# q and k loaded as pairs of tokens, one transpose per half, fillers in banks of their own, and a new order

## The chip, the cores and the metric

The kernel runs on one core of one Trainium2 chip. The metric is the device time of one execution in microseconds, the median of three runs. The engines are named as in the profile: PE is TensorE, DVE is VectorE, ACT is ScalarE, POOL is GpSimd, SP is SyncE (it issues most of the DMAs; ScalarE can issue some).

## The reference, cut to what matters

Attention over four batches of eight heads, 768 tokens and 64 columns a head. Each token sees its neighbours within 15 tokens, and 24 block keys (the maximum of k over 32 tokens) with the block means of v. The result, as 3072 rows of 512, goes through a feed-forward layer with 2048 columns.

```python
k_sum = k.reshape(B, H, nb, block, D).max(axis=3)
v_sum = v.reshape(B, H, nb, block, D).mean(axis=3)
scores_l = scale * np.matmul(q, k.transpose(0, 1, 3, 2))
mask_l = np.abs(pos[:, None] - pos[None, :]) < window
scores_s = scale * np.einsum('bhsd,bhnd->bhsn', q, k_sum) + np.log(block)
scores_all = np.concatenate([np.where(mask_l, scores_l, -1e9), scores_s], axis=-1)
# softmax over scores_all, times [v, v_sum]
...
h = x @ w_in
g = h - np.tanh(h)
return (g @ w_out).astype(np.float32)
```

## The kernel before, in words

The unit of work is a half of a batch, `u` of 8 (384 tokens, three tiles of 128), and a group `g` of four heads (two groups). For each (batch, group), `load_qk` fetches q and k in four pieces each of 192 KB on 128 partitions, and `turn` turns every piece with two transposes of VectorE into `qT` and `kT`, which hold columns on partitions. In the transposed tiles the tokens of a piece lie 24 apart. `top` takes the block maxima of k on VectorE and puts copies of them among the keys. `scores` is 48 multiplications into four PSUM banks, `softmax` works on pairs of heads `p` (four blocks for a half: two in each group): a minimum with the mask on VectorE, exponentials on ScalarE, the inverse of the sums, a scaling on any of three engines. `transpose_probs` turns the probabilities on TensorE (a `p turn`, seen as `ident,prob`), `values` multiplies them with v (`probT,vw`). The probabilities live in a ring of three buffers. The block means of v come from `sum_chunks` on TensorE, with the columns of a small constant tile (`wh`).

The feed-forward layer runs behind it in units (u, f), f being one of 16 column blocks: `moe_in` (`pH<-o,wf` in the first half), the activation, and `moe_out` into three banks `pY`. The weights are converted and split into high and low parts on VectorE, ScalarE and GpSimd as the first halves run (`convert`).

The program is a list of tasks with engines and costs (`Plan`). For the program that runs here the order of the tasks is written out, `ORDER`, and so is the engine of each task that may run on several, `ON`. `follow` goes through the tasks in this order and keeps a clock of its own for each engine. Where a TensorE task would start later than TensorE is free, it puts in fillers before it, multiplications of the unit matrix `ident` with itself (`keep_warm`), as many as its own costs say fit in the gap. Before, a filler counts as 0.214 us with a gap of 0.1, fillers stand anywhere in the first 100 us (`WARM`), and they write the bank `pS1`, which the scores use as well (`warm_bank`).

A second program behind a branch repeats the work in another way when a check at the end of the first asks for it; it did not run here.

Of the kernel before, what the change touches and what calls it, by code (L numbers as in the profile page):

```python
# [23 lines left out]
WARM = 100.0  # L24

# [64 lines left out]
class Plan:  # L90

    SEEN = {PE: 0.2, ACT: 0.19, DVE: 0.16, POOL: 0.1, SP: 0.85}
    QUEUE = 3.0
    LEAVES = {"scores": 0.105, "values": 0.105, "top turn": 0.17, "key turn": 0.105, "mean turn": 0.19, "sum": 0.105, "seen turn": 0.08}  # L100

    def __init__(self):
        self.tasks, self.rings, self.place, self.banks, self.count = [], {}, {}, set(), {}
        self.writer, self.readers, self.touch, self.first = {}, {}, {}, {}

    def ring(self, tag, bufs, base):
        self.place[base] = (self.rings.setdefault(tag, []), bufs)

    def add(self, kind, costs, go, r=(), w=()):
        t = Task()  # L110
        t.index, t.kind, t.costs, t.go = len(self.tasks), kind, costs, go
        n = self.count[kind] = self.count.get(kind, -1) + 1
        t.name = kind, n
        t.after, t.order = set(), set()
        t.banks = {key[0] for key in (*r, *w)} & self.banks
        self.tasks.append(t)
        for key in r:
# [7 lines left out]
        for base in dict.fromkeys(key[0] for key in (*r, *w)):  # L125
# [15 lines left out]
            self.touch.setdefault(base, []).append(t)  # L141
        t.after.discard(t)
        t.order.discard(t)
        t.order -= t.after
        return t

    def follow(self, idle):

        tasks = [self.tasks[n] for n in ORDER]
        free = dict.fromkeys((PE, DVE, ACT, POOL, SP), 0.65)  # L150
        dma, held, left = 0.0, {DVE: 0.0, POOL: 0.0}, 0.0
        clock, used, seen, done = Clock(), {}, {}, []
        begin = None
        for t in tasks:
            e = next(iter(t.costs)) if len(t.costs) == 1 else {"D": DVE, "A": ACT, "P": POOL, "S": SP}[ON[t.index]]
            assert all(a in seen for a in (*t.after, *t.order)), t.name
            t.engine, t.cost = e, t.costs[e]
            now = max([free[e]] + [seen[a] for a in t.after] + [at for b in t.banks for a, at in used.get(b, {}).items() if a != e])
            if e == PE:
                cost, go = idle  # L160
                if now > free[PE]:
                    begin = begin or tasks[0].out + self.SEEN[POOL]
                    free[PE] = max(free[PE], min(now, begin))
                while free[PE] < WARM and now - free[PE] > 2 * cost + 0.1:
                    d = Task()
                    d.after, d.order, d.go, d.engine, d.start = (), (), go, PE, free[PE]
                    d.out = clock.run(free[PE], cost)
                    free[PE] = d.out + 0.1
                    done.append(d)
                now = max(now, free[PE])  # L170
                t.cost += left if t.kind in ("in", "out") else 0.0
                left = self.LEAVES.get(t.kind, 0.0)
            elif SP in t.costs:
                now = max(now, dma - self.QUEUE)
            elif e == POOL:
                now = max(now, held[DVE])
                held[POOL] = now + t.cost
            elif e == DVE and t.kind in HELD:
                now = max(now, held[POOL])
                held[DVE] = now + t.cost  # L180
            t.start = now
            if SP in t.costs:
                t.out = free[e] = now + t.issue
                t.moves = max(dma, now + t.ahead)
                dma = t.moves + t.cost
                seen[t] = dma + self.SEEN[SP]
            else:
                t.out = free[e] = clock.run(now, t.cost) if e == PE else now + t.cost
                seen[t] = t.out + self.SEEN[e]
            for b in t.banks:  # L190
                used.setdefault(b, {})[e] = t.out + self.SEEN[e]
            done.append(t)
        return done

    def schedule(self, idle):
# [50 lines left out]
        while total:  # L246
# [20 lines left out]
            if e == PE and idle is not None:  # L267
                cost, go = idle
                if now > free[PE]:
                    free[PE] = max(free[PE], min(now, getattr(tasks[0], "out", now) + self.SEEN[POOL]))  # L270
                while free[PE] < WARM and now - free[PE] > 2 * cost + 0.1:
                    d = Task()
                    d.after, d.order, d.behind = tasks[:1], (), ()
                    d.start, d.engine, d.go = free[PE], PE, go
                    d.out = clock.run(free[PE], cost)
                    free[PE] = d.out + 0.1
                    done.append(d)
                now = max(now, free[PE])
# [61 lines left out]
def program(  # L340
# [14 lines left out]
    P = 128  # L355
# [393 lines left out]
    def raw_buf(which, b, g, j):  # L749
# [9 lines left out]
        if base not in made_by:  # L759
            buf(base, tag, [P, 4, JQ, D])  # L760
# [567 lines left out]
```

## Time and profile before

| | us |
|---|---|
| median of three runs | 665.31 |
| the three runs | 663.7, 665.31, 667.69 |
| the profiled execution | 663.14 |
| its span, first to last instruction | 661.4 |
| TensorE busy | 637.0 |
| VectorE busy | 469.8 |
| ScalarE busy | 452.8 |
| mean granted TensorE clock | 0.989 of full |

The span is a single core's. Busy times are sums over the whole span; the views by stretch tell where they lie. All work is recorded by one helper, line 57 of the kernel, so rows are told apart by their tiles. [...]

### The profile page before, as it was taken

How to read it: one execution, taken by the hardware profiler on the slowest of the kernel's cores; microseconds unless marked ns; L12 is line 12 of the kernel's file. 1: busy time of each engine (PE TensorE's matmuls, PEld its weight loads, DVE VectorE, ACT ScalarE, POOL GpSimd, SP SyncE). 2: the span in 40 equal slices, each digit the busy share in tenths (PEclk: the TensorE clock that was granted, in tenths of full speed). 3: DMA queues.
4: the chain of work that ended last, by engine and by line, in shares of the span. 5: the costliest groups of instructions: out<-in, count | busy, mean ns of one | idle time of the engine just before them, and what ended most of it. 6: DMA issues, size and time to landing. Idle time of an engine off the chain costs nothing.

```text
span 661.4 us, 15152 instructions
## 1 busy us (share of the span) xinstructions
PE 637.0 (96%) x5323; PEld 534.8 (81%) x5323; DVE 469.8 (71%) x1395; ACT 452.8 (68%) x1357; POOL 165.5 (25%) x240
## 2 busy tenths in 40 slices
PE   6789899999999999999999999999999999999997
PEld 6665556678889789999887889999888899999885
DVE  7879999999999894648768884457678844232363
ACT  1568888978898765554789865555798853444874
POOL 1111310214301412215354422211443203202311
PEclk9789999999999999999999999999999999999999
DMA  8648777865577776667534255557424045355101
GB/s 279 192 138 234 204 223 228 249 195 170 166 256 263 242 247 205 208 214 214 157 120 140 68 177 179 171 171 238 136 79 124 33 160 183 135 188 164 43 7 51
DMA packets 103329, 113.25 MB, mean 171 GB/s; under 512 B 43984, under 2 KB 71120, under 8 KB 103248
## 3 DMA queue, kind: packets, MB, share of 16 engines
q1 hardware_dynamic: 102240, 110.53, 53.3%
q10 hardware_dynamic: 1008, 1.70, 0.7%
q8 instruction: 43, 0.70, 0.4%
q14 instruction: 38, 0.31, 0.2%
HBM read 88.87 MB, written 20.97 MB: 166 GB/s over the span
## 4 chain that ended last, share of the span: by engine, by line
PE 76%; DVE 12%; DMA 7%; issue 2%; ACT 2%; POOL 1%; SPq 1%; DVEq 0%; POOLq 0%; ACTq 0%
PE pY L57 34%; PE pH L57 33%; PE pS L57 6%; DVE tmp L57 3%; PE pX L57 3%; DVE wf L57 2%; DMA wraw<-in_moe_w_out_dram 2%; DMA wraw<-scr 2%; DVE qT L57 1%; DVE prob L57 1%; DVE wraw L57 1%; DMA tmp<-in_v_dram 1%; DMA wh<-in_v_dram 1%; DVE kT L57 1%; DMA wraw<-in_moe_w_in_dram 1%
## 5 line engine op out<-in xcount | busy, mean ns | idle before, releaser
L57 ACT ACTIVATE prob<-prob,stat 128x120 f32<-128x120 f32 x296 | 109.6, 385 | 43.3 <-DVE stat L57 40.4
L57 PE MATMUL pH<-wf,wraw 128*128 128x384 f32 x552 | 116.2, 338 | 0.6 <-DMA wraw<-scr 0.4
L57 PE MATMUL pY<-wl,gh 128*128 128x512 f32 x288 | 113.4, 394 | 0.1
L57 PEld LDWEIGHTS pH<-wf,wraw 128*128 128x128 f32 x552 | 97.6, 188 | 6.8 <-ACT gu L57 0.6
L57 PE MATMUL pY<-wh,gh 128*128 128x512 f32 x204 | 84.5, 414 | 0.2 <-DVE gh L57 0.2
L57 PE MATMUL pY<-wh,gl 128*128 128x512 f32 x204 | 80.9, 396 | 0.0
L57 PE MATMUL pY<-wg,gh 128*128 128x512 f32 x168 | 68.8, 409 | 0.0
L57 PE MATMUL pY<-wg,gl 128*128 128x512 f32 x168 | 66.7, 397 | 0.2 <-DVE gl L57 0.2
L57 ACT ACTIVATE gu<-gu 128x384 f32<-128x384 f32 x128 | 65.5, 519 | 2.0
L57 PE MATMUL pH<-o,wf 128*128 128x384 f32 x188 | 65.9, 446 | 0.2 <-DVE wf L57 0.2
L57 PEld LDWEIGHTS pY<-wl,gh 128*128 128x128 f32 x288 | 54.2, 188 | 9.9 <-DVE wl L57 0.6
L57 POOL TENSOR_TENSOR gl<-gu,gh 128x384 fp32r<-128x384 f32 x29 | 30.3, 1046 | 119.3 <-ACT gh L57 79.6
L57 PE MATMUL pH<-wg,wraw 128*128 128x384 f32 x288 | 56.1, 338 | 0.1
L57 PEld LDWEIGHTS pH<-wg,wraw 128*128 128x128 f32 x288 | 50.7, 188 | 3.2 <-DMA wraw<-scr 0.6
L57 POOL TENSOR_TENSOR gu<-gu,gt 128x384 f32<-128x384 f32 x32 | 33.4, 1046 | 75.6 <-ACT gu L57 57.9
L57 ACT ACTIVATE gv<-pH 128x384 f32<-128x384 f32 x43 | 20.9, 487 | 37.5 <-PE pH L57 35.9
L57 PEld LDWEIGHTS pH<-o,wf 128*128 128x128 f32 x188 | 34.6, 191 | 14.5 <-issue 1.0
L57 PEld LDWEIGHTS pY<-wh,gl 128*128 128x128 f32 x204 | 38.2, 187 | 9.5 <-DVE gl L57 0.9
L57 ACT ACTIVATE gt<-gu 128x384 f32<-128x384 f32 x48 | 25.0, 520 | 29.9 <-DVE gu L57 28.3
L57 PEld LDWEIGHTS pY<-wh,gh 128*128 128x128 f32 x204 | 38.4, 188 | 7.2 <-issue 1.2
L57 PE MATMUL pY<-wf,gh 128*128 128x512 f32 x108 | 44.2, 439 | 0.0
L57 ACT ACTIVATE gu<-pH 128x384 f32<-128x384 f32 x46 | 22.3, 485 | 23.9 <-PE pH L57 23.6
(208 smaller groups left out, 1480.5 us busy)
## 6 DMA issues: line engine op xcount, KB each, us to landing
wraw<-scr SPq DMA_DIRECT2D x72, 512.0 KB
wraw<-in_moe_w_in_dram SPq DMA_DIRECT2D x16, 512.0 KB
wraw<-in_moe_w_out_dram SPq DMA_DIRECT2D x16, 512.0 KB
scr<-wraw SPq DMA_DIRECT2D x16, 512.0 KB
wraw<-scr SPq DMA_DIRECT2D x24, 256.0 KB
vw<-in_v_dram SPq DMA_DIRECT2D x60, 80.0 KB
raw<-in_q_dram SPq DMA_DIRECT2D x24, 192.0 KB
raw<-in_k_dram SPq DMA_DIRECT2D x24, 192.0 KB
```

What stands on the lines that cost most here:

```text
L57: return lambda *args, **kwargs: self._tc.keep_in_program_order(op(*args, **kwargs))
```

## The change

1. `load_half` takes the place of `load_qk`: one half (384 tokens) of q or k for a group comes in four DMAs of 96 KB, one for each head on 32 partitions (heads in the order 0, 2, 1, 3), in runs of 512 bytes, which are two tokens. One transpose of 768 elements turns the half. Neighbouring results lie two elements apart. For batch 0 these DMAs may go on ScalarE's queue as well. Raw halves lie in three tiles (`wg0`, `wg1`, `wg4`) for batch 0; the others share a ring `raw` of one buffer, where there were two.
2. The later half of q in batch 0 is loaded later; scores of a half wait for its own half of q alone.
3. Fillers write the banks `pY2` (up to the second scores) and `pS0` (between the first values and the third scores), cost 0.111 in the plan with no gap, and have no limit in time.
4. The mask is built on ScalarE (copies) and GpSimd (constants) and no longer on VectorE; the zeros of `kT` and `vw` are set on GpSimd.
5. Another weight group, other places for late tiles, other DMA costs in the plan, and so a new `ORDER` and `ON`.

```diff
-WARM = 100.0
-ORDER = [6, 28, 29, 7, 14, 15, 22, 23, 24, 0, 1, 3, 25, ...
+ORDER = [...
@@ follow
-                while free[PE] < WARM and now - free[PE] > 2 * cost + 0.1:
+                if spot == 1:
+                    free[PE] = max([free[PE]] + [min(now, at) for a, at in used.get(rest[3], {}).items() if a != PE])
+                while spot < 2 and now - free[PE] > 2 * cost + 0.1:
...
-                    d.out = clock.run(free[PE], cost)
-                    free[PE] = d.out + 0.1
+                    d.out = free[PE] = clock.run(free[PE], cost)
...
+                if t is rest[0] or t is rest[2]:
+                    spot = 2
+                elif t is rest[1]:
+                    spot = 1
@@ kernel
-    JQ = NB // 4
+    JH = U // 64
-    TURN_COST = 0.53
+    TURN_COST = 0.9
-    warm_bank = pp.tile([P, 512], F32, name="pS1", tag="pS1", bufs=1)
+    warm = {tag: pp.tile([P, 512], F32, name=tag, tag=tag, bufs=1) for tag in ("pY2", "pS0")}
...
-    do("const", DVE, 2.0, make_mask, r=[(("blk",), 1)], w=[MASK])
+    do("const", ACT, 2.6, make_mask, r=[(("blk",), 1)], w=[MASK])
+    do("const", POOL, 0.5, make_mask_sums, w=[(("mask",), 1)])
+    do("const", ACT, 0.45, make_mask_ends, r=[MASK, (("mask",), 1)], w=[(("mask",), 2)])
+    do("const", POOL, 0.2, make_mask_edges, w=[(("mask",), 2)])
...
+    def raw_buf(lazy):
+        if lazy or not raw_slots:
+            base = buf(("raws", len(plan.tasks)), "raw", [P, JH, 2, D])
+            return (lambda: at(base)), (base, 0)
...
+    def load_half(which, b, g, j, lazy=True):
+        to = qk_base(b, g)[which == "k"]
+        x, (base, n) = raw_buf(lazy)
+        for h in (0, 2, 1, 3):
+            src = (q if which == "q" else k)[b, HG * g + h, U * j:U * (j + 1)].rearrange("(j b r) d -> b j (r d)", j=JH, r=2)
+            dma(which + " load", lambda e, h=h, src=src: e.dma_start(x()[32 * h:32 * h + 32].rearrange("p j r d -> p j (r d)"), src), 32 * JH * 2 * D * 4, 2 * D * 4, w=[(base, (n, h))], both=b == 0)
+        do(which + " turn", DVE, TURN_COST, lambda: turn(which, x(), at(to), j), r=[(base, (n, h)) for h in range(HG)], w=[(to, j)])
+
+    def turn(which, x, to, j):
+        if which == "q":
+            x = x.rearrange("p j r d -> p (j r d)")
+            out = bass.AP(tensor=to.tensor, offset=to.offset + U * j, ap=[list(to.ap[0]), [64, JH], [1, 2], [S, 2], [2, 32]])
+        else:
+            x = bass.AP(tensor=x.tensor, offset=x.offset, ap=[list(x.ap[0]), [32, 4], [2 * D, JH], [1, 32]])
+            out = bass.AP(tensor=to.tensor, offset=to.offset + col(U * j), ap=[list(to.ap[0]), [1, 2], [KT, 2], [N2, U // LOC], [2, LOC // 2]])
+        vector.transpose(out, x)
...
-        do("scores", PE, 1.3, go, r=[*((qT, j) for j in range(4)), *((kT, x) for x in (0, 1, 2, 3, "zero", "top", "sums"))], w=[(x, i) for x in banks for i in range(NT)])
+        do("scores", PE, 1.3, go, r=[(qT, u % 2), *((kT, x) for x in (0, 1, "zero", "top", "sums"))], w=[(x, i) for x in banks for i in range(NT)])
...
+    for g in range(NG):
+        when(1 + 4 * g, load_half, "q", 0, g, 1)
...
-    def keep_warm():
-        tensor.matmul(warm_bank[:, 512 - P:], ident, ident, start=True, stop=True)
+    def keep_warm(tag):
+        return lambda: tensor.matmul(warm[tag][:, 512 - P:], ident, ident, start=True, stop=True)
...
-    for t in plan.schedule((0.214, keep_warm)):
+    first = [[t for t in plan.tasks if t.kind == kind] for kind in ("scores", "values")]
+    plan.fill = first[0][1], first[1][0], first[0][2], ("px", 0, 0)
+    for t in plan.schedule((0.111, [keep_warm(tag) for tag in warm])):
```

Three places of the new order follow. A number behind a name tells the buffer, an `x` how many like it follow in a row.

TensorE between the first scores and the second, before the change: the fillers are `ident` alone, `ident,prob` turns probabilities, and `wg_144,oo` is the first multiplication of the second scores.

```order
L57 MATMUL pS_73<-ident 128x128 x17
L57 MATMUL pS_405<-ident,prob 120x128 x4
L57 MATMUL pS_73<-ident 128x128 x2
L57 MATMUL pS_405<-ident,prob 120x128 x2
L57 MATMUL pS_73<-ident 128x128 x12
L57 MATMUL pH<-wg_144,oo 64x120
```

The same place after the change.

```order
L55 MATMUL pY_73<-ident 128x128 x41
L55 MATMUL pS_74<-ident,prob 120x128 x4
L55 MATMUL pY_73<-ident 128x128 x3
L55 MATMUL pS_74<-ident,prob 120x128 x2
L55 MATMUL pY_73<-ident 128x128 x33
L55 MATMUL pH<-wg_139,oo 64x120
```

The useful rows stand in the same order; there are 77 fillers in place of 31. Ahead of the first scores the rows of fillers are 3, 38 (between the two v sums) and 8, where they were 20, 5 and 1. Between the second and the third scores four rows of 4, 3, 4 and 4 fillers are added.

VectorE from its first transpose on, before the change (`kT` and `qT` are group 0):

```order
L57 STREAM_TRANSPOSE kT<-wh_100 128x6x8x4 x2
L57 MEMSET vw 16x256
L57 STREAM_TRANSPOSE qT<-wh_105 128x6x32 x2
L57 STREAM_TRANSPOSE qT<-wh_109 128x6x32 x2
L57 STREAM_TRANSPOSE kT<-wh_113 128x6x8x4 x2
L57 MEMSET wg_138 16x256
L57 STREAM_TRANSPOSE kT<-wh_140 128x6x8x4 x2
L57 MEMSET wg_144 128x2x16 x2
L57 STREAM_TRANSPOSE kT<-wh_136 128x6x8x4 x2
L57 TENSOR_REDUCE kT<-kT 128x24 x2
L57 COPY kT<-kT 128x2x8x24
L57 STREAM_TRANSPOSE qT<-wh_207 128x6x32 x2
```

After the change, from its first transpose to the first minimum of the softmax (`oo` is the q of group 1):

```order
L55 STREAM_TRANSPOSE kT<-wg_134 128x2x2x4x48
L55 STREAM_TRANSPOSE kT<-wg_123 128x2x2x4x48
L55 TENSOR_REDUCE kT<-kT 128x24 x2
L55 STREAM_TRANSPOSE qT<-wg_123 128x6x2x2x32
L55 COPY mean<-pH 24x64 x3
L55 STREAM_TRANSPOSE oo<-wg_279 128x6x2x2x32
L55 COPY mean<-pH 24x64
L55 ISA prob,stat<-pH,mask 128x120
```

Four transposes stand ahead of the first minimum where there were eighteen, and none of the mask's copies.

SyncE's queue at its start, before:

```order
L57 DMA wh_100<-in_k_dram 128x384
L57 DMA wh_105<-in_q_dram 128x384
L57 DMA wh_109<-in_q_dram 128x384
L57 DMA wh_113<-in_k_dram 128x384
L57 DMA wh_136<-in_k_dram 128x384
L57 DMA wh_140<-in_k_dram 128x384
L57 DMA gt<-in_v_dram 128x384
```

and after:

```order
L55 DMA gu<-in_v_dram 128x384
L55 DMA gt<-in_v_dram 128x384 x2
L55 DMA gu<-in_v_dram 128x384 x2
L55 DMA wg_134<-in_k_dram 32x6x128 x3
L55 DMA wg_144<-in_v_dram 16x4x64
L55 DMA wg_123<-in_k_dram 32x6x128
```

The pieces of v for the sums stand first on this queue now; five pieces of k and q are issued from ScalarE at the same time, ahead of its table load and the mask's copies. On GpSimd `ident` is made behind the two parts of the constant tile, where it was made first.

## Rows read from the trace of the kernel before

**Rows 1.** The page: span, and busy time of the matrix engine.

```profile
span 661.4 us, 15152 instructions
...
PE 637.0 (96%) x5323; PEld 534.8 (81%) x5323; DVE 469.8 (71%) x1395; ACT 452.8 (68%) x1357; POOL 165.5 (25%) x240
```

**Rows 2.** Busy time by stretch: start:end, length, engines (instructions), clock, DMA share, GB/s.

```profile
0.00:54.13 54.13, 40.66 (x559) 34.18 (x559) 42.97 (x156) 25.97 (x91) 7.94 (x26) 0.87 0.70 210
54.13:160.00 105.87, 101.21 (x951) 67.56 (x952) 101.82 (x286) 89.79 (x276) 19.11 (x22) 1.00 0.71 213
160.00:240.00 80.00, 78.68 (x700) 67.27 (x700) 73.88 (x224) 67.60 (x206) 20.55 (x37) 1.00 0.71 233
240.00:656.90 416.90, 416.49 (x3117) 365.76 (x3115) 250.81 (x731) 268.89 (x786) 117.94 (x155) 1.00 0.45 144
```

**Rows 3.** TensorE's waits from 54.13 to 656.9: total, times, longest.

```profile
PE pS L57 <- DVE prob L57: 1.5, 2, 1.3
PE pS L57 <- DMA wh<-in_v_dram: 1.1, 1, 1.1
```

**Rows 4.** TensorE's fillers: timeline 21:22.8 and 30:32 (start, length), and their group.

```profile
20.79 1.95 PE L57 MATMUL pS<-ident 128*128 128x128 f32 x16
...
29.44 2.93 PE L57 MATMUL pS<-ident 128*128 128x128 f32 x12 [1.44 <-DVE stat L57]
...
L57 PE MATMUL pS<-ident 128*128 128x128 f32 x134 | 21.2, 320 | 7.8 <-ACT probT L57 3.2 <-DVE stat L57 3.1 <-POOL ident L57 1.5
```

**Rows 5.** TensorE's timeline up to the third scores: start, length, [idle before <-releaser].

```profile
1.50 6.50 PE L57 MATMUL pS<-ident 128*128 128x128 f32 x40 [1.50 <-POOL ident L57]
...
15.88 0.43 PE L57 MATMUL pH<-kT,qT 32*64 32x120 f32 x1 [2.21 <-DVE qT L57]
...
18.51 4.22 PE L57 MATMUL pS<-ident 128*128 128x128 f32 x34
23.99 0.65 PE L57 MATMUL pS<-ident,prob 128*120 128x128 f32 x4 [1.26 <-POOL prob L57]
...
33.77 0.31 PE L57 MATMUL pH<-wg,oo 32*64 32x120 f32 x1
...
42.31 0.61 PE L57 MATMUL pY<-ident,prob 128*120 128x128 f32 x4
...
49.14 0.94 PE L57 MATMUL pY<-ident,prob 128*120 128x128 f32 x6
...
54.13 0.31 PE L57 MATMUL pH<-kT,qT 32*64 32x120 f32 x1 [0.19 <-ACT gu L57]
```

**Rows 6.** VectorE's timeline ahead of the first scores.

```profile
3.31 0.91 DVE L57 STREAM_TRANSPOSE kT<-wh 128x192 f32<-128x192 f32 x2 [2.23 <-DMA wh<-in_k_dram]
...
9.22 1.74 DVE L57 TENSOR_REDUCE kT<-kT 128x24 f32<-128x768 f32 x2
...
12.60 0.26 DVE L57 COPY mask<-wh 64x16 f32<-64x16 f32 x2
...
15.08 1.14 DVE L57 STREAM_TRANSPOSE qT<-wh 128x192 f32<-128x192 f32 x2
```

**Rows 7.** SyncE's queue and GpSimd's constants in the first 5 us.

```profile
0.91 0.38 SPq L57 DMA_DIRECT2D wh<-in_k_dram  x1
...
3.70 0.43 SPq L57 DMA_DIRECT2D gt<-in_v_dram  x1
...
3.28 0.83 POOL L57 TENSOR_SCALAR_AFFINE_SELECT wh<-wh 128x192 f32<-128x192 f32 x2
```

**Rows 8.** Busy time in two stretches at the low clock (columns as in rows 2).

```profile
42.80:46.20 3.40, 3.40 (x31) 2.51 (x30) 2.56 (x11) 2.37 (x10) 0.00 (x0) 0.50 0.15 34
...
15.46:18.88 3.42, 3.00 (x97) 2.67 (x98) 1.96 (x7) 0.00 (x0) 0.00 (x0) 0.50 0.79 230
```

**Rows 9.** VectorE's transposes of later batches: busy us, mean ns, idle before.

```profile
L57 DVE STREAM_TRANSPOSE qT<-raw 128x192 f32<-128x192 f32 x48 | 27.0, 665 | 2.9 <-DMA raw<-in_q_dram 2.9
...
L57 DVE STREAM_TRANSPOSE kT<-raw 128x192 f32<-128x192 f32 x48 | 22.2, 543 | 1.2 <-DMA raw<-in_k_dram 1.2
```

More of the change, by code (lines that the diff above doesn't have):

```diff
@@ L266, in schedule @@
                 able[a].remove(t)
[L267 to L278, printed above, removed]
             if e == DVE and t.kind in HELD:
@@ L497, in make_mask, with make_mask_sums, make_mask_ends, make_mask_edges @@
                 f, rows = sums_at(2 * i + half), slice(64 * half, 64 * half + 64)
-                vector.tensor_copy(mask[rows, i, 0:f], x[rows, 0:f])
-                vector.tensor_copy(mask[rows, i, f + NB:N2], x[rows, f:LOC])
-                vector.memset(mask[rows, i, f:f + NB], 8 * LOG32)
-        vector.tensor_copy(mask[:, 3], mask[:, 0])
-        vector.tensor_copy(mask[:, 4], mask[:, 2])
-        vector.memset(mask[0:64, 3, 0:PAD], -8 * BIG)
-        vector.memset(mask[64:P, 4, N2 - PAD:N2], -8 * BIG)
+                copy(scalar, mask[rows, i, 0:f], x[rows, 0:f])
+                copy(scalar, mask[rows, i, f + NB:N2], x[rows, f:LOC])
+    def make_mask_sums():
+        for i in range(NT):
+            for half in range(2):
+                f, rows = sums_at(2 * i + half), slice(64 * half, 64 * half + 64)
+                gpsimd.memset(mask[rows, i, f:f + NB], 8 * LOG32)
+    def make_mask_ends():
+        copy(scalar, mask[:, 3], mask[:, 0])
+        copy(scalar, mask[:, 4], mask[:, 2])
+    def make_mask_edges():
+        gpsimd.memset(mask[0:64, 3, 0:PAD], -8 * BIG)
+        gpsimd.memset(mask[64:P, 4, N2 - PAD:N2], -8 * BIG)
     def make_blk():
@@ L744, in finish_v @@
         do("mean out", ACT, 0.28, lambda: scalar.activation(mean[32 * g:32 * g + NB], at(ps)[:NB, :HG * D], AF.Copy, scale=1.0 / 32), r=[(ps, 0)], w=MEANS[g])
-    raw_slots = [f"wh{n}" for n in (0, 1, 3, 5, 14, 16, 18, 20)] + [("raws", tag, n) for tag in ("wg0", "wg1") for n in range(4)]
-    def raw_buf(which, b, g, j):
-        if b:
-            base = buf((which + "r", len(plan.tasks)), "raw", [P, JQ, D], F32, 2)
+    raw_slots = [(tag, n) for tag in ("wg0", "wg1", "wg4") for n in range(2)]
@@ L1186, in means, with qk @@
         when(m, place_v, b, g, "pS1")
-    def qk(m, b, g):
-        when(m, load_qk, b, g)
+    def qk(m, b, g, halves=(0, 1)):
+        for j in range(2):
+            when(m, load_half, "k", b, g, j)
         when(m, top, b, g)
+        for j in halves:
+            when(m, load_half, "q", b, g, j)
     def sums(m, b, g):
@@ L1198, in program @@
         load_part(0, n, next(v_tags))
[L1199 to L1206 removed]
+    for g in range(NG):
+        load_half("k", 0, g, 0, False)
+        load_half("q", 0, g, 0, False)
+        load_half("k", 0, g, 1, False)
+        top(0, g)
+        load_v(0, g)
+        if g == 0:
+            for n in range(HG):
+                load_part(0, HG + n, next(v_tags))
     for i in range(2 * NF):
@@ L1214, in program @@
         block(0, g)
+    for g in range(NG):
+        when(1 + 4 * g, load_half, "q", 0, g, 1)
     if small_only:
```

76 lines of the change are left out of this document (25 added, 51 removed).

## The prediction

> **What bounds the kernel now.** I read the page's busy lines first, then busy time and granted clock by stretch, then TensorE's waits, and then the timelines of TensorE and VectorE over the first 54 us. The page says TensorE is busy 637.0 of 661.4 us [rows 1]. The stretches say where it is not [rows 2]. Up to 54.13 us, where the scores of the second half of batch 0 start (the "third scores" below), it is busy 40.66 of 54.13. From there to its last matmul it lacks 4.66 us up to 160, 1.32 up to 240 and 0.41 after that, 6.4 in all, at a granted clock of 1.00. What is left of the span is a tail of 4.5 us. So there are two places to win or lose in: the front, and at most 6.4 us behind it. VectorE stands at 101.82 of 105.87 us between 54.13 and 160, so it is the second bound there; the waits of that stretch name it for 1.5 us and a v load for 1.1 [rows 3].
>
> Of the 40.66 us before 54.13, 21.2 are fillers, multiplications that nobody reads [rows 4]. The timeline of the front [rows 5] reads: fillers, the v sums, scores at 15.88, 17 fillers, first turn of the probabilities at 23.99, 12 fillers from 29.44 on [rows 4], second scores (group 1) at 33.77, turns of the third and fourth block at 42.31 and 49.14, third scores at 54.13. The first scores waited 2.2 us for VectorE, for a q transpose that stood behind the mask work [rows 5, 6].
>
> **What a filler costs.** One filler leaves two records in the trace (20 in the order, 40 in the first row of rows 5). At the high clock 16 records run in 1.95 us; with the length of the last one (about 0.28) taken off, 15 starts are 0.111 us apart, so one filler is 0.223 us [rows 4]. In a stretch that lies mostly at the low level, 12 records take 2.93 us, up to 0.49 a filler. The old planner counts 0.214 and a gap of 0.1 for one, the new one 0.111 and no gap. That is a record, not a filler: the new program fills each gap of its plan about twice over. Fillers stand in TensorE's own queue, so whatever follows them waits whether its data are there or not.
>
> **Part 1, the front.** The order has 126 fillers on the first bank (3, then 38, 8, 41, 3, 33) and 15 on the second, against 67 before, and the same useful work up to the third scores. Step by step: v is now first in SyncE's queue with k beside it on ScalarE's. Before, the first k piece was on VectorE at 3.31 [rows 6]; five pieces of 192 KB at the 210 to 260 GB/s of the first stretch would put the v pieces at 5 to 7.5, and I take 6.0. The constant behind the fillers is now made last on GpSimd, where the last of that work ended at 4.1 [rows 7], so the first three fillers cost nothing. Then 0.7 (sum) + 38 x 0.223 = 8.5 + 0.7 + 8 x 0.223 = 1.8, and 1.7 because the first few us will be granted the low level (0 to 3.4): first scores at 19.4, against 15.88. Their data should be ready at about 13: the mask work of 12.60 to 15.08 is off VectorE and one transpose takes the place of eight, so nothing but the fillers holds them. Scores 1.5 and 41 fillers, 9.1: first turn at 30.0 instead of 23.99. The softmax is ready some 8.1 us behind the scores (15.88 to 23.99), at 27.5, so again fillers decide. Turns 1.0 and 36 fillers, 8.0: second scores at 39.0 instead of 33.77.
>
> From here on the chain is softmax, not fillers. Before, the third block's turn came 42.31 - 33.77 = 8.5 after the second scores and the fourth's 6.8 behind it, with VectorE also doing the group's transposes and conversions; the third scores came 5.0 later. The third block cannot start its softmax before the second one's turns, about 2 us behind the second scores, and needs about 6.4 from there; the fourth the same; then 5.0 less what the cold clock took: 39.0 + 2 + 6.4 + 6.0 + 5.0 = 58.4. The floor without any wait is counted from the work: useful 40.66 - 21.2 = 19.5, of which 3.4 and 3.0 us ran at a granted 0.50 [rows 8] and would take half, so 16.3; 138 fillers 30.8; start 6.0; cold start 1.7: 54.8. The ceiling is the chain with the old 8.5 and 6.8: 39.0 + 8.5 + 6.8 + 5.0 = 59.3, and up to 61 with a longer cold start. **Front: +4 us** (third scores at 58; +0.7 to +7).
>
> **Part 2, transposes.** Before: 128 transposes of 128x192, 0.665 us for q and 0.543 for k in the 96 of the later batches [rows 9], about 65 us of VectorE. After: 32 of 768 elements. By the old price per element they would take 2.66 and 2.17, 77 us in all. The old ones write every 24th element, though, the new ones every second; the nearest row with dense rows is the maximum over 768 elements, 1.74 us for two [rows 6], 0.87 each. I take 0.87, 28 us (28 to 77). VectorE then wins about 37 us, some 10 of them between 54 and 240 (32 transposes, 19 us, become ten, 9 us).
>
> The trace shows 2.8 to 3.5 ns for each element of a transposed row [rows 9]. [...]
>
> **Part 3, the stretch from 54 to 240.** The useful work behind the third scores is the same. VectorE's relief can end waits only of the 6.4 us; the v load's 1.1 stays. Half of the rest is behind softmax on VectorE and ScalarE. **Gain 3 us** (0 to 6). Also here: the later loads go through one buffer in place of two, in twice as many DMAs of 96 KB.
>
> **Part 4, answered at once.** Mask work on ScalarE lies ahead of its first exponentials, behind five DMA issues on the same queue; eight more issues stand between it and the exponentials, about 4 us at SyncE's pitch of 0.47 (six issues from 0.91 to 3.70 [rows 7]). The exponentials need the first scores, so the cover is the fillers ahead of these; bare, both would be 5 us. The sums' copy into k goes to GpSimd, idle there. The later half of q in batch 0 is wanted only at 58. The tail is not touched.
>
> **Sum.** The profiled execution took 663.14 (span 661.4 and 1.7 around it): 663.1 + 4 - 3 = 664.1. The median of the runs shown, 665.31, is 2.2 above it, so **666.3**, 0.15% above before; a measurement of this kernel tells about 0.5%, 3.3 us, from no change.
>
> **Rivals.** *Faster: the front gives nothing away.* If the v pieces land at 5, the clock rises at once and VectorE, rid of its transposes, takes the third and fourth softmax in the shadow of the other work, the third scores come at the floor, 54 to 55, and 5 of the 6.4 us go: 663.1 + 0.5 - 5 = 658.6, by the median 660.8. For it: VectorE was 42.97 of 54.13 us busy there. Against: both softmaxes must be covered by about 17 us of work. It turns faster from the front's loss less than 1.5 us on. Chance 0.22. *Slower: the transpose keeps its price per element.* Then a group's four take 9.7 us, as its sixteen did (8 x 0.665 + 8 x 0.543 = 9.7), VectorE stays full from 54 to 240 and part 3 gives nothing; the front's loss of 4 to 5 stays: 668 to 669, by the median 670 to 671. It decides from 1.6 us a transpose up. For it speaks that no row shows such a transpose at speed. Chance 0.18. *Slower by the loads.* With one buffer, each of the 24 later half-tensors waits for the transpose of the one before it, and SyncE's queue, with the weights behind it, waits too. The first row of rows 3 that names a DMA is 1.1 us; if a third of the 24 cost TensorE half as much, that is 4.4, 668.5, by the median 671. Against: weights are three buffers ahead. Chance 0.12. [...]
>
> **Chances.** Forecast 0.48 (its own range 662.5 to 669), faster 0.22, slower 0.30. The range takes the floor of the front with most of part 3 at its low end, and a full loss of the front and slow loads at its high end: 657 to 674.
>
> **What would show it.** In the changed kernel's trace: rows of 76, 82 and 66 filler records back to back before first scores, first turn and second scores; first scores near 19.4, second near 39, third near 58; transposes of 0.87; VectorE busy 10 us less between 54 and 240 and TensorE idle there 3 us instead of 6. It is wrong if a filler leaves one record or half the time, if useful work waits in front of the fillers, or if the third scores start before 54.

## The result and the profile after

The changed kernel takes 672.67 us (median of 11 runs, 668.37 to 680.01) against 665.21 for the kernel before beside it (11 runs, 662.14 to 668.33). The ratio is 1.0105, 95% interval 1.0077 to 1.0132, without the run of 680.01, which is a slow one. So the change costs 1%, where 0.15% was forecast: inside the predicted range (657 to 674), but outside the forecast's own 662.5 to 669. The profiled execution of after took 673.41, with a span of 671.7 and the same 1.7 around it.

The page of after, which answers to [rows 1]:

```profile
span 671.7 us, 15484 instructions
...
PE 650.4 (97%) x5471; PEld 551.4 (82%) x5471; DVE 450.6 (67%) x1272; ACT 453.6 (68%) x1371; POOL 158.6 (24%) x253
```

VectorE has 19.2 us less to do and TensorE 13.4 us more, on the same multiplications that anybody reads. Where that lies is in the timeline of TensorE up to the third scores, to be laid beside [rows 5] (start, length, operation, how many, [idle before and releaser]):

```profile
4.16 1.65 PE L55 MATMUL pY<-ident 128*128 128x128 f32 x6 [4.16 <-POOL ident L55]
...
7.56 0.32 PE L55 MATMUL pH<-gu,wh 128*32 128x64 f32 x1 [0.53 <-DMA gu<-in_v_dram]
...
8.97 11.06 PE L55 MATMUL pY<-ident 128*128 128x128 f32 x76
...
20.78 2.05 PE L55 MATMUL pY<-ident 128*128 128x128 f32 x16
22.76 0.31 PE L55 MATMUL pH<-kT,qT 32*64 32x120 f32 x1
...
24.32 9.42 PE L55 MATMUL pY<-ident 128*128 128x128 f32 x82
33.58 0.60 PE L55 MATMUL pS<-ident,prob 128*120 128x128 f32 x4
...
34.99 7.53 PE L55 MATMUL pY<-ident 128*128 128x128 f32 x66
42.45 0.31 PE L55 MATMUL pH<-wg,oo 32*64 32x120 f32 x1
...
60.13 0.31 PE L55 MATMUL pH<-kT,qT 32*64 32x120 f32 x1
```

The fillers end where the first scores (rows of 76 and 16, with the second v sum between them), the first turn (82) and the second scores (66) begin, with no idle time in brackets: TensorE comes to each of these from its own fillers, not from a wait. The third scores start at 60.13, 6.0 later than before.

The data of the first scores had been there for a while. VectorE's timeline has the transposes for them:

```profile
9.82 1.84 DVE L55 STREAM_TRANSPOSE kT<-wg 128x768 f32<-128x768 f32 x2 [9.82 <-DMA wg<-in_k_dram]
...
15.32 0.98 DVE L55 STREAM_TRANSPOSE qT<-wg 128x768 f32<-128x768 f32 x1 [1.81 <-DMA wg<-in_q_dram]
```

The q transpose ends at 16.30, the scores start at 22.76. For 6.5 us after the last operand was ready TensorE does nothing but fillers and the 0.8 us of the second v sum.

Busy time by stretch (columns as in [rows 2]):

```profile
60.13:160.00 99.87, 95.14 (x924) 63.38 (x924) 92.61 (x259) 88.44 (x270) 18.22 (x22) 1.00 0.75 214
160.00:240.00 80.00, 76.59 (x692) 67.30 (x691) 68.27 (x196) 66.50 (x212) 21.52 (x38) 0.98 0.69 221
240.00:667.18 427.18, 424.67 (x3153) 372.27 (x3151) 257.33 (x714) 270.05 (x786) 111.59 (x160) 1.00 0.48 148
```

TensorE's idle time is length less busy time: 4.73, 3.41 and 2.51 us, 10.65 in all, against 4.66, 1.32 and 0.41 before, 6.4. The useful work is the same, 596.4 us of busy time in both. So behind the third scores after loses 4.3 us more, although VectorE is down at 92.61 of 99.87 in the first of the stretches. The four largest waits there (total, times, longest):

```profile
PE pH L55 <- DVE qT L55: 2.0, 1, 2.0
PE pH L55 <- DVE wf L55: 1.6, 2, 1.3
PE pX L55 <- DVE probT L55: 1.4, 1, 1.4
PE pH L55 <- DMA wraw<-scr: 1.2, 2, 0.7
```

They are not those of [rows 3]; the v load's 1.1 and the 1.5 for `prob` on VectorE are gone, and waits for a q transpose, converted weights, probabilities and a weight load have come. The tail is 4.5 us as before. The 10.3 us between the spans are thus 6.0 in the front and 4.3 behind it. The medians lie only 7.5 us apart: the traced execution of before was 2.1 below its median, that of after 0.7 above. So this account is good to 2 or 3 us.

### The profile page after: what moved, and what is told of

Its sections match the earlier page's. It is cut to its first block, busy times and chain, and to the rows that moved or that the text cites. A ratio compares the mean times of both kernels' runs of the same rounds, so it can differ in the third digit from the quotient of the medians.

```text
span 671.7 us, 15484 instructions
## 1 busy us (share of the span) xinstructions
PE 650.4 (97%) x5471; PEld 551.4 (82%) x5471; DVE 450.6 (67%) x1272; ACT 453.6 (68%) x1371; POOL 158.6 (24%) x253
## 4 chain that ended last, share of the span: by engine, by line
PE 68%; DVE 9%; DMA 8%; ACT 6%; POOL 3%; issue 2%; SPq 2%; ACTq 0%; DVEq 0%; POOLq 0%
PE pY L55 34%; PE pH L55 29%; PE pS L55 3%; PE pX L55 2%; DVE tmp L55 2%; DVE wraw L55 2%; SPq L55 2%; ACT prob L55 2%; POOL tmp L55 2%; DMA wraw<-scr 2%; DMA tmp<-in_v_dram 1%; DMA raw<-in_k_dram 1%; DVE prob L55 1%; DMA raw<-in_q_dram 1%; ACT o L55 1%
## 5 line engine op out<-in xcount | busy, mean ns | idle before, releaser
L55 PE MATMUL pH<-wf,wraw 128*128 128x384 f32 x552 | 112.4, 338 | 0.9 <-DMA wraw<-scr 0.7
L55 PE MATMUL pH<-wg,wraw 128*128 128x384 f32 x432 | 85.9, 339 | 1.4 <-DVE o L55 0.9
L55 PE MATMUL pY<-wh,gh 128*128 128x512 f32 x204 | 83.1, 408 | 0.0
L55 PEld LDWEIGHTS pH<-wg,wraw 128*128 128x128 f32 x432 | 75.7, 188 | 5.9 <-DVE o L55 1.4
L55 ACT ACTIVATE gv<-pH 128x384 f32<-128x384 f32 x37 | 18.1, 489 | 40.8 <-PE pH L55 40.8
L55 POOL TENSOR_TENSOR gu<-gu,gt 128x384 f32<-128x384 f32 x24 | 24.4, 1019 | 83.6 <-ACT gu L55 60.6
L55 DVE COPY gv<-pH 128x384 f32<-128x384 f32 x35 | 19.5, 556 | 34.1 <-PE pH L55 34.0
```

Of the source, the lines that this page charges most:

```text
L55: return lambda *args, **kwargs: self._tc.keep_in_program_order(op(*args, **kwargs))
```

## Experiments on the front: the fillers

The theory: what starts late in the front starts late because TensorE has to get through fillers first, twice too many of them, since the plan prices one at 0.111 us and it takes 0.223. Its rivals: the fillers are what holds the clock up and so earn their time, or the loads and the softmax chain hold the front in any case. Three runs tell them apart: the right price in the new kernel, no fillers at all in it, and the wrong price in the old kernel.

**The true price.** 54 fillers in place of 141.

```diff
-    for t in plan.schedule((0.111, [keep_warm(tag) for tag in warm])):
+    for t in plan.schedule((0.223, [keep_warm(tag) for tag in warm])):
```

> The changed kernel with one number other: a filler counts 0.223 us in the plan instead of 0.111, so 53 fillers stand in the program instead of 141, at the same places. Theory A (the fillers in TensorE's own queue set the front): 14 fillers ahead of the first scores instead of 49, so these start when q's transpose is done, at 16.3 to 17.5 instead of 22.76; second scores at 34 to 36 instead of 42.45; third scores at 53 to 55 instead of 60.13; the stretch behind stays as it is, so the time falls by 5 to 7 us, to 666 to 668. Rival B (what fillers cost they give back by the clock): with fewer fillers the granted clock falls to 0.5 in the gaps, the useful work runs at half speed there, the third scores come at 58 or later and the time falls by less than 2 us.

662.23 us, ratio 0.998 (0.9945 to 1.0015). TensorE's timeline:

```profile
15.56 0.28 PE L55 MATMUL pH<-kT,qT 32*64 32x120 f32 x1 [0.95 <-DVE qT L55]
...
17.08 4.51 PE L55 MATMUL pY<-ident 128*128 128x128 f32 x38
...
31.63 0.31 PE L55 MATMUL pH<-wg,oo 32*64 32x120 f32 x1
...
48.04 0.31 PE L55 MATMUL pH<-kT,qT 32*64 32x120 f32 x1 [0.18 <-ACT gt L55]
```

The first scores now wait for their q transpose, as they should, and the third come 12.1 us earlier than in after and 6.1 earlier than before. The span falls by 9.2. One number makes the difference between slower and the same.

**No fillers at all.**

```diff
-                while spot < 2 and now - free[PE] > 2 * cost + 0.1:
+                while False:
```

> The changed kernel without any filler. Theory A: nothing holds the useful work but data and the clock. First scores at 16.3, at the low clock and so 1.3 us longer; the front's multiplications, some 16 us at the high clock, run mostly at the low one, with the softmax waits of about 6 us a block in between; third scores at 55 to 58 and a few us behind them still at the low level, time 668 to 671, between the one with 53 fillers and the changed kernel. Rival B (the fillers earn their time by the clock): third scores at 60 or later, time 673 or more.

662.49 us, ratio 0.9966 (0.9946 to 0.9987): 0.3% below before, and not to be told apart from the true price's 662.23. The timeline:

```profile
15.88 0.43 PE L55 MATMUL pH<-kT,qT 32*64 32x120 f32 x1 [0.85 <-DVE qT L55]
...
23.58 1.11 PE L55 MATMUL pS<-ident,prob 128*120 128x128 f32 x4 [5.00 <-ACT prob L55]
...
37.47 0.67 PE L55 MATMUL pY<-ident,prob 128*120 128x128 f32 x4
...
48.04 0.31 PE L55 MATMUL pH<-kT,qT 32*64 32x120 f32 x1 [1.04 <-ACT gt L55]
```

Four turns of probabilities take 1.11 us at 23.58 and 0.67 at 37.47. The first multiplication of the first scores takes 0.43 us, as in before, where the granted clock was 0.50 around it [rows 5, 8]; that of the second scores, at 27.82, takes 0.42, where after has 0.31. So without fillers TensorE runs at a lower level up to 27.82 at least, more than half of the front, and yet the third scores start at the same 48.04. TensorE is busy 25.39 of these 48.04 us and waits for softmax in between; a slower multiplication ends in time that was idle anyway. So the fillers earn nothing here, and the rival that they pay through the clock falls. (The old kernel was not run without fillers.)

**The wrong price in the old kernel.** 195 fillers in place of 67, all else as before.

```diff
-                    d.out = clock.run(free[PE], cost)
-                    free[PE] = d.out + 0.1
+                    d.out = free[PE] = clock.run(free[PE], cost)
...
-    for t in plan.schedule((0.214, keep_warm)):
+    for t in plan.schedule((0.111, keep_warm)):
```

> The kernel before with the changed kernel's price of a filler (0.111 and no gap instead of 0.214 and 0.1), nothing else: 195 fillers instead of 67, on the old bank. Theory A: 53 + 15 + 5 fillers ahead of the first scores, which come at 20 to 22 instead of 15.88; 88 more ahead of the second scores, 43 to 46 instead of 33.77; third scores at 62 to 67 instead of 54.13; time 8 to 13 us above before, 673 to 678. Rival (fillers only fill waits that are there): third scores within 2 us of 54, time within 2 us of before.

679.05 us, ratio 1.0213 (1.0182 to 1.0244).

```profile
1.49 14.64 PE L57 MATMUL pS<-ident 128*128 128x128 f32 x106 [1.49 <-POOL ident L57]
...
22.54 0.31 PE L57 MATMUL pH<-kT,qT 32*64 32x120 f32 x1
...
47.22 0.31 PE L57 MATMUL pH<-wg,oo 32*64 32x120 f32 x1
...
68.78 0.31 PE L57 MATMUL pH<-kT,qT 32*64 32x120 f32 x1
```

The third scores move from 54.13 to 68.78 by this edit alone. The wrong price costs the new kernel about as much as the whole change (ratio 1.0105 against 0.998) and the old one 2.1%.

## Experiments behind the third scores

With the true price the new kernel reaches the third scores 6.1 us earlier than before and yet its ratio is 0.998, a gain of little over 1 us. Behind the third scores it takes 609.94 us against 602.77; its idle time there is 11.1, in the kernel without fillers 13.3. Another 2.4 us are busy time (598.8 against 596.4); the granted clock averages 0.98 from 48.04 to 160 and 0.98 from 160 to 240, where before has 1.00 from 54.13 on [rows 2]. Theories: the single buffer of the ring `raw`; single places in the order; VectorE (that its relief is worth nothing, or that it is still the bound); the loads' shape.

**Two raw buffers** (the changed kernel, its fillers unchanged; a table that only the closing check of the kernel reads is shortened to make room, and that check sees the last 48 sums alone).

```diff
-            base = buf(("raws", len(plan.tasks)), "raw", [P, JH, 2, D])
+            base = buf(("raws", len(plan.tasks)), "raw", [P, JH, 2, D], F32, 2 if small_only else 1)
```

> The changed kernel with two buffers instead of one for the halves of q and k that are loaded later. To make room, the table of sums for the closing check has 48 columns instead of 128, so the check sees the last 48 sums only. Theory C (the single buffer makes loads wait for transposes, and TensorE waits behind them): the wait of 2.0 us for a q transpose at 178.7 goes, TensorE's idle time behind the third scores falls from 10.6 to 7 or 8 us, the time by 2 to 3.5 us, to 669 to 670.5. Rival D (the new order as a whole leaves less slack, and q and k have little part in it): the idle time stays at 9.5 to 11 us, the time at 671.5 to 673.5. The front is not touched: third scores at 60.

672.9 us, ratio 1.0125 (1.0095 to 1.0155), the same as after. Idle time behind the third scores is 10.68 (after: 10.65), and the wait for a q transpose is still 1.8:

```profile
PE pX L55 <- ACT probT L55: 2.8, 2, 2.2
PE pH L55 <- DVE wf L55: 2.4, 4, 1.0
PE pH L55 <- DVE qT L55: 1.8, 1, 1.8
```

In after's trace the chain load, transpose, next load is plain to see (a q transpose at 173.30 that waited 3.53 for its load, the next at 179.58). With a second buffer it is there all the same, at 174.56 and 180.49. The buffer was not what spaced it.

**Three places of the order** (with the true price). Two additions for the weights on VectorE (tasks 1033 and 1034) move behind the work that waited 1.4 and 2.0 us in after, and one v load for the block means (997) behind four q loads on SyncE.

```diff
-ORDER = [... 998, 1033, 931, ... 1000, 1034, 982, ... 976, 997, 996, ...
+ORDER = [... 935, 1033, 936, ... 982, 1034, 1009, ... 974, 997, 924, ...
```

> The changed kernel with a filler's price of 0.223 (as in e1_true_cost, the base of this run) and three tasks moved in the written order, nothing else: the two mixes of w_out's sums that wait for GpSimd (VectorE) go behind the copies of the turned probabilities and behind the second q transpose, and one load of v chunks goes behind the four q loads. Theory D (the new order is planned too tightly and its places cost the stretch behind the third scores): TensorE's two waits at 165 and 168 us of e1_true_cost, 1.4 for a copy of the probabilities and 2.0 for the q transpose, go or shrink to under 1.5 together, the rest stays: 2 us less than e1_true_cost, 660 to 661, ratio to before 0.994 to 0.996. Rival C (loads of q and k through one buffer set the time of those scores whatever the order): the q transpose is not earlier, at most the 1.4 goes: ratio 0.997 to 0.999.

663.6 us, ratio 0.9995 (0.9976 to 1.0015): no gain. The wait of 1.4 for `probT` is gone, others have grown:

```profile
PE pH L55 <- DVE wf L55: 3.3, 3, 2.4
PE pH L55 <- DMA wraw<-scr: 2.9, 4, 1.4
PE pH L55 <- DVE qT L55: 2.4, 1, 2.4
```

**Order and buffers together** (the last two, and four more q loads ahead of another v load, 999, and the late half of q on SyncE alone).

```diff
-ORDER = [... 977, 999, 1322, ... 1007, 978, 979, 981, 980, 1001, ...
+ORDER = [... 977, 978, 979, 981, 980, 999, 1322, ...
...
-... both=b == 0)
+... both=b == 0 and not lazy)
```

> e5_order with two buffers for the later halves of q and k (the closing check sees the last 48 sums only, to make room), the second half's q loads of batch 2, group 0, ahead of the last load of v chunks, and the late q halves of batch 0 on SyncE's queue instead of ScalarE's, where they wait inside ScalarE's own work for a buffer. Theories C and D together: the waits around 81 to 83 us (2.0 us, for ScalarE's exponentials) go as well: TensorE idle 6 to 7 us behind the third scores instead of 11, 3.5 to 4.5 us less than e1_true_cost, ratio 0.990 to 0.993. If only the order counts: as e5_order.

665.85 us, ratio 1.0018 (0.9994 to 1.0041); idle time 14.2, with 4.9 in five waits for weight loads and 2.6 for ScalarE in their place. Each place that is mended by hand gives its time to another.

**Does VectorE matter? More of it** (true price; each of the 24 transposes of batches 1 to 3 is issued twice).

```diff
-lambda: turn(which, x(), at(to), j)
+lambda: [turn(which, x(), at(to), j) for _ in range(2 if lazy and b and small_only else 1)]
```

> e1_true_cost with every transpose of batches 1 to 3 issued twice: 24 more of 0.97 us on VectorE, 23 us, most of what the change takes off it. Theory D: VectorE is not what TensorE waits for behind the third scores; only the transposes on the chain load, transpose, next load count, so the time rises by 1 to 4 us (ratio to before 1.000 to 1.004). Rival (VectorE's relief is what the change lives by): the time rises by 6 us or more, ratio 1.007 or higher.

673.4 us, ratio 1.0157 (1.0127 to 1.0188). The stretch behind the third scores:

```profile
47.60:666.38 618.78, 599.27 (x4765) 500.91 (x4765) 438.69 (x1192) 425.25 (x1267) 151.01 (x219) 1.00 0.53 165
```

VectorE is busy 438.69 there, 18.8 more than with the true price alone (419.94), and TensorE idles 19.5 in place of 11.1. VectorE's time is not free.

**Less of it in the old kernel** (one transpose per piece in batches 1 to 3 in place of two: 48 fewer; the scores of these batches are then not the reference's).

```diff
-        for db in range(2):
+        for db in range(1 if b and small_only else 2):
```

> The kernel before with half of the transposes of batches 1 to 3 left out (the second 32 columns of each head keep what batch 0 left there, so the scores of these batches are not the reference's): 48 fewer, 29 us of VectorE less, in the old order. By the prediction's part 3 VectorE's relief would end 3 of the 6.4 us of TensorE's waits there: ratio 0.994 to 0.997. Theory D: waits are set by the order and by loads, not by VectorE's load: ratio 0.997 to 1.001 and 5 to 6.5 us idle behind the third scores.

658.52 us, ratio 0.9923 (0.9894 to 0.9953).

```profile
53.59:652.17 598.58, 594.41 (x4765) 501.44 (x4765) 411.43 (x1193) 425.36 (x1266) 158.86 (x214) 1.00 0.53 170
```

VectorE is 15.1 us down there and TensorE's idle time falls from 6.4 to 4.2. This is the relief that the change was forecast to bring, in the old arrangement, and it is worth 0.8%. Idle time is only half of it: TensorE's busy time also falls by 2.0 us on the same 4765 records (596.38 to 594.41), which the trace doesn't explain.

**Less of it in the new kernel** (true price; the transposes of batches 1 to 3 turn half of their elements, so the scores are not the reference's).

```diff
-            x = x.rearrange("p j r d -> p (j r d)")
+            n = JH // 2 if half else JH
+            x = x[:, :n].rearrange("p j r d -> p (j r d)")
```

> e1_true_cost with the transposes of batches 1 to 3 cut to half of their elements (the other half of q and k keeps what was there, so the scores of these batches are not the reference's): 24 transposes of about 0.49 instead of 0.97, 11.5 us of VectorE less. If VectorE still sets the stretch behind the third scores (twice the transposes, 23 us, cost 10 to 12 us): 4 to 6 us less than e1_true_cost, ratio to before 0.989 to 0.992, TensorE idle 6 to 8 us there. If the change has taken off VectorE all that TensorE waits for, and the rest of its waits are the order's and the chains': within 1.5 us of e1_true_cost, ratio 0.996 to 0.999, idle 10 us or more.

662.81 us, ratio 0.9984 (0.9958 to 1.0011): no more than the true price alone.

```profile
49.13:657.03 607.90, 596.47 (x4765) 501.55 (x4765) 409.42 (x1168) 424.85 (x1267) 151.64 (x219) 1.00 0.55 168
...
L55 DVE STREAM_TRANSPOSE qT<-raw 128x384 f32<-128x384 f32 x12 | 6.9, 575 | 5.3 <-DMA raw<-in_q_dram 5.3
```

This window and the one before it are the two to lay side by side. VectorE has the same work in both, 409 and 411 us. The old arrangement idles 4.2 us, the new one 11.4. So some 7 us belong to what else the change moved behind the third scores (the order, the choice of engines, the loads), and not to VectorE's load. The other traces agree: with these two, three of the old order idle 4.2 to 6.4 us there, ten of the new one (without the doubled transposes) 10.7 to 14.2. Up to the change's own transposes VectorE's time matters; below that, something else ends last.

## Experiments on the loads

**Long runs** (true price; the same 96 KB on 32 partitions, in runs of 3072 bytes in place of 512, tokens misplaced).

```diff
-.rearrange("(j b r) d -> b j (r d)", j=JH, r=2)
+.rearrange("(b n) d -> b (n d)", b=32)
```

> e1_true_cost with the loads of q and k reading the same 96 KB on the same 32 partitions in one run of 3072 bytes for each partition instead of six of 512, so tokens stand in other places and the scores are not the reference's. Theory C1 (short runs make the loads slow, and TensorE and VectorE wait behind them): q of the first scores lands 2 us earlier or more, these start at 14 or before; behind the third scores TensorE is idle 8 us or less instead of 11; ratio to before 0.989 to 0.993 against 0.998. Rival D (the loads' speed doesn't matter there, the order and VectorE's work set the stretch): ratio 0.996 to 0.999, idle 10 to 12 us.

662.38 us, ratio 0.9979 (0.9953 to 1.0004), idle time 13.1 behind the third scores. The runs of 512 bytes cost nothing that shows.

**All partitions** (true price; the half in four DMAs of 128, 64, 128 and 64 KB on 128 partitions, tokens misplaced).

```diff
-        for h in (0, 2, 1, 3):
+        flat = (q if which == "q" else k)[b, HG * g:HG * (g + 1)].rearrange("h (n r) d -> (h n) (r d)", r=2).rearrange("(n p) x -> p n x", p=P)
+        for h, c0, c1 in ((0, 0, 2), (2, 2, 3), (1, 3, 5), (3, 5, 6)):
```

> e1_true_cost with each half of q and k loaded by four DMAs of 128 partitions (128, 64, 128 and 64 KB) instead of four of 32 partitions (96 KB), the same runs of 512 bytes, from other tokens, so the scores are not the reference's. Theory C2 (32 partitions at a time make the loads slow): first scores at 14 or before, TensorE idle 8 us or less behind the third scores, ratio 0.989 to 0.993. Rival D: as e1_true_cost, first scores at 15.5 to 17, ratio 0.996 to 0.999.

661.17 us, ratio 0.9945 (0.9924 to 0.9966), against 0.9979 for the long runs on the same chip; the intervals overlap. The first q transpose, with long runs and then with all partitions:

```profile
14.64 0.98 DVE L55 STREAM_TRANSPOSE qT<-wg 128x768 f32<-128x768 f32 x1 [1.44 <-DMA wg<-in_q_dram]
```

```profile
13.15 0.98 DVE L55 STREAM_TRANSPOSE qT<-wg 128x768 f32<-128x768 f32 x1 [0.69 <-DMA wg<-in_q_dram]
```

With the true price alone it starts at 14.44, so 128 partitions win 1.3 us here, of the 13 to 15 that pass up to this transpose. Idle time behind the third scores stays at 11.4.

**No fillers and wide first loads together** (the right tokens: each half of batch 0 that is loaded at the start in six DMAs of 64 KB on 128 partitions).

```diff
-        for h in (0, 2, 1, 3):
+        for h, js in ((0, (0, 1)), (2, (2,)), (1, (3, 4)), (3, (5,))) if not lazy else [(h, ()) for h in (0, 2, 1, 3)]:
...
+... [e.dma_start(x()[:, n].rearrange("p r d -> p (r d)"), wide[n]) for n in js] ...
```

> The changed kernel without fillers (as e2_no_fillers), and the halves of q and k that are loaded first in batch 0 come in six DMAs of 64 KB on 128 partitions instead of four of 96 KB on 32; nothing is left out. If the 1.2 us that wide loads won at the first scores holds: first scores at 14 to 15, third scores at 46 to 47, ratio to before 0.993 to 0.996 (without the wide loads 0.9966). If the two more DMA issues for each half eat it: first scores at 16 or later, ratio 0.996 to 0.999.

672.88 us, ratio 1.0129 (1.0097 to 1.0161): it was meant as a better version and throws away all that the fillers' removal had won. The third scores are at 59.58 again. TensorE's waits up to 46 us:

```profile
PE pH L55 <- DMA gv<-in_v_dram: 10.6, 2, 10.1
PE pS L55 <- ACT prob L55: 10.2, 1, 10.2
```

Both waits stand behind queues of issues. On SyncE's, the four k pieces ahead of the later v pieces take 6.13 us to issue, and the first of these v pieces leaves at 15.12; without the wide loads it left at 8.54:

```profile
4.90 6.13 SPq L55 DMA_DIRECT2D wg<-in_k_dram  x4
...
15.12 0.47 SPq L55 DMA_DIRECT2D gv<-in_v_dram  x1
```

So the second v sum waits until 18.79; the q transpose, late for its load too, starts at 21.33, and the first scores, which wait for it, at 22.45. On ScalarE's queue stand issues (ACTq) ahead of the first exponential (ACT):

```profile
17.61 5.14 ACTq L55 DMA_DIRECT2D wg<-in_q_dram  x5
...
22.79 7.55 ACTq L55 DMA_DIRECT2D wg<-in_k_dram  x8
30.39 0.39 ACT L55 ACTIVATE prob<-prob,stat 128x120 f32<-128x120 f32 x1 [15.91 <-DMA wg<-in_k_dram]
```

These 13 issues take 12.7 us, about 0.98 each, and the exponentials come only at 30.39. In after five issues fit ahead of the exponentials:

```profile
14.98 2.70 ACTq L55 DMA_DIRECT2D wg<-in_k_dram  x5
...
24.82 0.40 ACT L55 ACTIVATE prob<-prob,stat 128x120 f32<-128x120 f32 x1 [14.38 <-DVE stat L55]
```

The number of issues is not the whole reason. Between 6 and 16 us the DMA engines move 88 GB/s with a busy share of 0.29, where the kernel without wide loads (second row) moves 224 with 0.86:

```profile
6.00:16.00 10.00, 2.06 (x48) 1.43 (x44) 0.87 (x1) 4.77 (x19) 0.00 (x0) 1.00 0.29 88
```

```profile
6.00:16.00 10.00, 3.96 (x102) 3.03 (x110) 4.86 (x7) 4.30 (x19) 0.65 (x3) 1.00 0.86 224
```

A share of 0.29 is 4.6 of the 16 engines on average. Either these DMAs, whose source steps over the four heads outermost, were slow in themselves, and the long issues are queues that wait for them, or the issues themselves were slow; no run separates the two. The run above on all partitions, whose source has the 128 partitions outermost, moves 217 GB/s up to its third scores (46.66 us), this one 172 up to its own (59.58). Whether wide loads at the start are worth having stays open, then: this run shows the way they were cut, not the width.

## Why the prediction was right and wrong

**The filler, right.** Two records each, 0.226 us where 0.223 was taken: 82 records from 24.32 to 33.58. The rows of 76, 82 and 66 records stand where they were forecast, and the theory that they hold the front is shown from three sides: the true price takes 12.1 us off it, none takes the same, and the wrong price in the old kernel adds 14.7.

**Part 1, right in its mechanism up to the second scores, short by 2 us** (+4 forecast, +6.0 measured, inside +0.7 to +7). Two terms were mis-sized. The v pieces were put at 6.0; the last of them was waited for until 7.56 and the sum ended at 9.0, where 6.7 was forecast. And the 38 fillers behind it took 11.06 us where 8.5 + 1.7 was allowed: they run at 11 or 12 records per 2 us up to 14 us and at 21 from there, so the slow start lasted longer. That made the first scores 22.76 and not 19.4; the second, 42.45, keep this 3.4 and no more, since the 41 and 36 fillers were sized rightly. From the second scores to the third 17.7 us passed, where 19.4 were forecast, and the mechanism was another: not the softmax chain but TensorE's own queue, with 15 fillers in it, since TensorE idles there only 1.04 us. (The forecast's sum for this stretch has 6.0 for the fourth block where its text says the same as the third's 6.4, and the full 5.0 without the cold clock's share; neither decides anything.) The data of the first scores were ready at 16.3 and not at 13, which fillers covered, as said; in the true-price kernel, without that cover, it is the 0.95 us that the first scores wait.

**Part 2, the transpose right, VectorE's gain too high.** 0.974 us for 768 elements, near the 0.87 taken and nowhere near 2.17 to 2.66:

```profile
L55 DVE STREAM_TRANSPOSE kT<-raw 128x768 f32<-128x768 f32 x12 | 11.7, 974 | 2.6 <-DMA vw<-in_v_dram 1.4 <-DMA raw<-in_k_dram 1.2
...
L55 DVE TENSOR_TENSOR gu<-gu,gt 128x384 f32<-128x384 f32 x52 | 29.8, 576 | 6.2 <-ACT gu L55 6.2
```

The rival by which the price per element stays falls. All 32 transposes take 31 us by their groups, where 128 took 65. VectorE as a whole is down by 19.2, not by 37. Some 4 us were handed back: the other groups of VectorE add up to 487.2 us where they were 483.3, though the mask's copies are gone. By the new choice of engines VectorE does 52 of the additions `gu<-gu,gt`, where it did 44 (25.1 us); other tasks went the other way. The rest, some 11 us, is that busy times of groups don't add up to that of the engine, since neighbours overlap in the records (in before a transpose starts at 8.53 and takes 0.48 us, the next starts at 8.86). Leaving out 48 of the 96 transposes that make up the 49.2 us of [rows 9] lowered VectorE's busy time behind the third scores by only 15.1.

**Part 3 is the step that failed.** A gain of 3 us was forecast behind the third scores (0 to 6), and a loss of 4.3 measured. The reasoning was: the same useful work, VectorE is the second bound, so its relief can only end waits. Its first half is borne out (relief in the old kernel takes idle time from 6.4 to 4.2, twice the transposes in the new one add 8.4). What it left out is that the new order and the new choice of engines re-deal every wait of this stretch, and that nothing in the trace of before could price them. That was counted as a gain with a floor at zero; the bound should have reached below zero, by how much no row of before could tell. At equal load of VectorE the new arrangement idles 7 us more, and that is shown. Which of its places cause it is not: not the single buffer, not the length of the runs, not three places of the order mended by hand, and little or none of it the partitions. That stays open. The start of the stretch decides little: new kernels whose third scores come at 47 to 49 idle 11 to 14 us behind them, those where they come at 58 to 60 idle 10.7 to 11.8, and the old one with the wrong price starts them at 68.78 and idles 6.1.

**Part 4, no cost, as forecast, and not the 5 us when bare either.** In the kernel without fillers, which lacks their cover, the first turn comes at 23.58, 7.7 us behind the first scores, where before it came 8.1 behind them [rows 5]: no cost of the mask work and the issues shows there.

**The rivals.** *Faster: the front gives nothing away* did not happen, since fillers were the bound; with these gone the front comes to 48.04, below the floor of 54 to 55, which had counted them as work. *Slower by the loads* had the right sign and nearly the right size (671 against 672.67), but its mechanism is not what happened: two buffers change nothing. With the true price the new kernel is not slower than before, so without the surplus fillers there would have been nothing to explain by the loads.

**Sum.** +4 - 3 was forecast and +6.0 + 4.3 measured, on 661.4 of span. The sign turned in part 3, which makes 7.3 of the 9.3 us of the miss; 2.0 are in part 1. That the time still lies inside 657 to 674 is luck in part: the high end was set by a full loss of the front, which came, and by slow loads, which the runs do not show.

## What to carry to other kernels

Before counting on work that is meant to keep an engine's clock up, leave it out once and look where the next useful instruction starts: here it stood in TensorE's own queue ahead of useful work (first scores at 22.76, their data ready at 16.30), the plan's price for it (0.111 us) was half of what it takes (0.226), and the version without any of it was as fast as the one with the right price (662.49 and 662.23 us). Relief of the second-busiest engine has to be weighed together with everything that the same edit re-orders, and a re-ordered stretch can lose as well as win. DMA issues on a computing engine's queue can hold up what stands behind them (here 13 of them took 12.7 us, and the exponentials came at 30.39, 2.7 us behind VectorE's first minimum), so whoever splits loads another way has to see first what rate they reach (88 GB/s against 224 here) and how long their issues hold the queue.

## What the runs showed of the hardware

A VectorE transpose of fp32 with results two elements apart took 0.974 us for 768 elements and 0.575 for 384, so 1.04 ns for an element more, with 0.18 us on top. With results 24 apart it was 2.8 to 3.5 ns an element, that part included [rows 9]; the second of two back to back added 0.37 to 0.48 us for 192 elements [rows 6], 1.9 to 2.5 ns an element.

The granted clock in these views does not show every slow stretch. The view of the kernel without fillers gives 1.00 over the whole front, while its instructions show the lower level: 1.11 us for four turns at 23.58 and 0.67 at 37.47, of the same shape. Durations of a known instruction are the better clock there:

```profile
0.00:48.04 48.04, 25.39 (x425) 17.55 (x425) 32.03 (x104) 27.66 (x104) 7.41 (x34) 1.00 0.79 214
```

A DMA issue has no one price here. On ScalarE it took 0.54 us in the row of five in after, 1.2 in the same kernel's row of three from 1.84 on, and 0.94 and 1.03 in the rows of eight and five where the loads were split finer; on SyncE it was 0.47 in [rows 7] and up to 1.5 in the finer split, whose loads moved at 88 GB/s.
